# State products of the first quarter split straight from PSUM, other quarters by stacked products, and a new order

## The chip, the cores and the metric

One core of a Trainium2 chip runs the kernel. Its engines are PE (matrix multiplication), DVE (vector), ACT (scalar functions), POOL (general) and SP, which here issues the DMAs. The metric is the device time of one execution in microseconds; lower is better. Times given for a kernel are the median of several executions, and the profile is one more execution, recorded by the hardware.

## The reference

```python
# x: (8, 8, 512, 64)  state: (8, 8, 32, 64)   batch, head, rows, D
scores = scale * x @ state^T;   a  = softmax(scores);   xread = a @ state
scores2 = scale * state @ x^T;  a2 = softmax(scores2);  sread = a2 @ x
y = concatenate([xread, sread], axis=2)          # 544 rows a head
rows = y.transpose(0, 2, 1, 3).reshape(8 * 544, 512)
h = rows @ w_in                                  # 512 x 2048
g = maximum(h, 0) + log1p(exp(-abs(h)))          # softplus
out = g @ w_out                                  # 2048 x 512
```

`w_in` and `w_out` come as 64-bit floating point and are turned into 32-bit words on the chip.

## The kernel before

**The products.** The kernel does not compute xread. Because xread @ w_in is the sum over heads of a times (state times the head's 64 rows of w_in), it first makes the *state product* V = state @ w_in of each batch (256 rows, head by state row, by 2048 columns), and then the hidden tile h.b.f (128 columns of h for batch b, 512 rows) from V and the softmax a. Every factor is split into a high part, rounded to the fast matmul format, and a low part, the rest (`split`: the high part is a cast, L293 on ACT, the low part a subtraction, L309 on DVE); a product takes three matmuls (high-high, high-low, low-high). A hidden tile has two groups of heads, so six matmuls. Softplus (`s`) and another split (`gh`, `gl`) follow, and four output products of three matmuls (`m.b.f.c`) with tile f of w_out (`Wh`, `Wl`) add into accumulators of one PSUM bank each.

**Four quarters.** w_in is treated in four quarters c of 512 columns, four hidden tiles each. Quarter pieces of w_in are loaded (`Li`), converted by three steps (`ch` on ACT, `cu` and `cr` on DVE: a scaled high word, the low word's bits by L341 or by the pair L344 and L345, and their union, L349), and stored for later (`Sw`). For quarters 0 and 1 the state products come from plain 32-bit matmuls (`V0` for batches 0 and 1, `V1` for batches 2 and 3, 128 rows of two batches by two heads). Batches 0 and 1 are copied from PSUM into a buffer Vk (`va`) and then split (`vh`, `vl`); batches 2 and 3 are copied out (`ve`), stored to DRAM (`Sv`) and loaded again in another layout (`F`). Quarters 2 and 3, and batches 4 to 7 of all quarters, use *stacked products*: a head's rows of w_in are split into a high and a low half, stacked in one operand R (`Rh`, `Rl`, L370), and multiplied by the high and the low part of the states of four batches (`P`, two matmuls, fast format); the result is evicted (`pe`), stored (`Sp`, vd<-px) and loaded back (`F`, Vf<-vd).

**Attention.** For batches 0 and 1 the scores (`Q`) are plain 32-bit matmuls of z, a block layout of the state, and xT, x transposed. DVE transposes the scores in blocks (`A`, L457), takes maxima (`M`, L458), POOL or DVE subtracts (`Ms`, L460), ACT takes the exponential (`m`, L461), DVE sums, adds EPS and inverts (`N`, L464 to L466), POOL or DVE multiplies (`Nm`, L470), DVE transposes back (`D`, L471), and a split gives aH and aL. The row maxima (`E`, L479 and L480) and the row exponentials (`e`) serve sread alone, which is needed at the end (tile 8 of h).

**The order.** `PLAN` is an order written out: each step's name, its engine (V and W are DVE with one or two instructions for the low words, A and C are ACT, G POOL, T PE, S SP), and the number of the buffer or PSUM bank of what it makes. Every engine works through its own instructions in that order and waits for what each needs. The batches' hidden tiles run in turns: batch 0 tiles 0 to 3, batch 1 tiles 0 to 7, batch 0 tiles 4 to 11, batch 1 tiles 8 to 15, batch 0 tiles 12 to 15, then batch 2 and so on. Sixteen records of matmuls on zeros (`h.idle`, eight matmuls, WARM, L744) stand at the very start, and transposes of the identity (`w`, L604) fill some places of PE's order. z of batches 0 and 1 is cleared by POOL (`zn`, L544); its two halves are copied in from a loaded buffer zf (`zc`).

```python
rs = slice(64 * (q % 2), 64 * (q % 2) + 64)
for b in range(2):
    op(f"va.{k}.{b}", "AV", [f"vp.0.{k}"], [f"Vk.{b}.{c}:{i}"],
       lambda e, k=k, b=b, c=c, q=q, cs=cs, rs=rs, n=n:
       copy(e, page(f"Vk.{b}.{c}", 2, 512)[rs, q // 2, cs], at(f"vp.0.{k}")[64 * b:64 * b + 64, 0:n]))
```

Of the kernel before, what the change touches and what calls it, by code (L numbers as in the profile page):

```python
# [8 lines left out]
F32 = mybir.dt.float32  # L9
F32R = mybir.dt.float32r  # L10
I32 = mybir.dt.int32
I64 = mybir.dt.int64
# [7 lines left out]
P = 128  # L20
# [8 lines left out]
WARM = 8  # L29
TURNS = ((0, 0, 4), (1, 0, 8), (0, 4, 12), (1, 8, 16), (0, 12, 16))  # L30
PACKED = (2, 3)
# [3 lines left out]
Lt.0:S:0 Lz.0:S:1 zn.0:G:0 Li.0.1:S:2 Lq.1:S:3 Li.0.3:S:4 Lq.0:S:5 Li.0.0:S:6 Li.0.7:S:7 Lo.0:S:0 Lo.1:S:1 Li.0.2:S:8 zc.0.0:V: zc.0.1:V: Q.0.0:T:0  # L35
ch.0.1:C:9 cu.0.1:W:10 cr.0.1:V: Sw.0.1:S: ch.0.3:A:11 cu.0.3:V:12 V1.0.1:T:1 E.0.0:V: Q.0.1:T:2 ve.0.1:A:13 cr.0.3:V: Sv.0.1:S: A.0.0:V:14 zn.1:G:15
ch.0.0:A:16 Lz.1:S:17 Lt.1:S:1 cu.0.0:V:18 ch.0.7:A:19 M.0.0:V: V0.0.3:T:3 Sw.0.3:S: w.25:T:4 A.0.1:V:20 Li.0.6:S:21 va.0.3.1:A:2 Ms.0.0:G: w.26:T:5
va.0.3.0:A:3 Li.0.5:S:22 w.27:T:6 E.0.1:V: Li.0.4:S:23 w.28:T:7 m.0.0:A: M.0.1:V: e.0.1:A:24 cr.0.0:V: N.0.0:V: Ms.0.1:G: w.32:T:1 Sw.0.0:S: V1.0.0:T:4
ch.0.2:C:25 V0.0.1:T:5 ve.0.0:A:26 cu.0.2:W:27 V1.0.3:T:3 m.0.1:A: cu.0.7:V:28 cr.0.2:V: va.0.1.1:A: cr.0.7:V: ve.0.3:A:29 N.0.1:V: zc.1.0:A: Nm.0.0:G:
V1.0.7:T:6 Sw.0.7:S: zc.1.1:A: va.0.1.0:A: w.40:T:7 Sv.0.0:S: e.0.0:A:30 V0.0.7:T:2 Lo.2:S:4 cu.o0:V:31 V0.0.0:T:1 D.0.0:V:32 ve.0.7:A:33 Sw.0.2:S:  # L40
Nm.0.1:G: V0.0.2:T:4 va.0.7.1:A: Sv.0.7:S: va.0.0.0:A: V1.0.2:T:3 va.0.0.1:A: Li.1.1:S:5 cu.o1:V:34 va.0.2.0:A: Q.1.1:T:5 ah.0.0:A:35 D.0.1:V:36
vh.0.0:G:37 va.0.7.0:A: al.0.0:V:38 ah.0.1:A:39 cu.0.6:V:40 ch.0.6:A:41 vl.0.0:V:42 Q.1.0:T:7 Sv.0.3:S: va.0.2.1:A: Li.1.3:S:6 cr.0.6:V: ch.0.4:A:43
cu.0.4:V:44 Lo.3:S:7 cu.0.5:V:45 ch.0.5:A:46 cr.0.4:V: Sw.0.6:S: ch.o0:A:47 cr.0.5:V: Sw.0.4:S: V0.0.4:T:0 ch.o1:A:48 A.1.0:V:49 al.0.1:G:50 V0.0.5:T:6
va.0.4.0:A: A.1.1:V:51 V0.0.6:T:1 va.0.4.1:A: va.0.5.0:A: M.1.0:V: h.0.1:T:2 va.0.5.1:A: ch.o2:A:52 va.0.6.0:V: Li.1.2:S:8 Ms.1.0:G: M.1.1:V:
va.0.6.1:A: vh.0.1:A:53 h.0.0:T:4 cr.o0:V: Li.1.0:S:9 vl.0.1:V:55 V1.0.4:T:0 cr.o1:V: s.0.1:A:54 h.0.2:T:6 s.0.0:A:56 cu.o2:V:57 ve.0.4:V:58 Ms.1.1:G:
wh.0:A:59 gh.0.0:A:60 V1.0.6:T:1 wl.0:V:61 h.0.3:T:2 wh.1:A:62 gl.0.0:V:1 gh.0.1:A:2 s.0.2:A:9 cr.o2:V: m.0.0.2:T:4 ve.0.6:A:4 wl.1:V:11 wh.2:A:6
# [210 lines left out]
def width(buf):  # L257
# [5 lines left out]
    if kind in ("xT", "po"):  # L263
        return 4
    if kind in ("o8", "x", "xs", "Wf", "Vk", "aa"):
        return 2
    return 2 if kind == "w8" and at[0] != "0" else 1


def rounded(buf):  # L270
# [543 lines left out]
```

## Time and profile before

| | us |
|---|---|
| median of 3 runs (671.3 to 672.15) | 672.12 |
| profiled execution | 673.18 |
| its span, first to last instruction | 671.4 |
| PE busy | 659.2 (98%) |
| DVE busy | 417.0 (62%) |
| ACT busy | 425.0 (63%) |
| POOL busy | 16.5 (2%) |

The page cuts the span into 40 slices of 16.8 us; each digit is the busy share of a slice in tenths. PE's and DVE's rows, with the other rows of the page left out:

```profile
PE   7899999999999999999999999999999999999997
...
DVE  4999999836987896354854476446736666322210
```

A timeline row has its start and its length in us, the engine, the line, the operation, out<-in by names, shapes and a count; in brackets stands how long the engine was idle before it and what ended that. A matmul's length in such a row includes its way through the pipeline, so lengths overlap; the distance between starts is what a matmul costs in a full stream. A plain 32-bit matmul shows as two records.

### The profile page before, as it was taken

The numbers are of one execution on the slowest core, as the hardware profiler recorded it, in microseconds if no ns is written. First come the engines' busy times: TensorE is split into PE (matmuls) and PEld (weight loads), VectorE is DVE, ScalarE is ACT, GpSimd is POOL, SyncE is SP. The second block draws the span as 40 slices with busy tenths as digits, with TensorE's granted clock in tenths as the row PEclk, the third lists the DMA queues.
The fourth block names the chain that finished last, engine by engine and source line by source line (L and its number), as shares of the span: only waits on it lengthen the run. The fifth ranks groups of instructions, "written<-read, shape, count | busy, mean of one in ns | idle before, by whom it ended". The sixth has DMA issues, their size and how long they took to land.

```text
span 671.4 us, 8968 instructions
## 1 busy us (share of the span) xinstructions
PE 659.2 (98%) x3036; PEld 540.2 (80%) x3036; DVE 417.0 (62%) x802; ACT 425.0 (63%) x751; POOL 16.5 (2%) x21
## 2 busy tenths in 40 slices
PE   7899999999999999999999999999999999999997
PEld 5567778888888788888888888888888888988886
DVE  4999999836987896354854476446736666322210
ACT  3979998877877686563864467456845747324322
POOL 2430000000000000000000000000000000000000
PEclk9999999999999999999999999999999999999999
DMA  8849677675063434521341122312073312103001
GB/s 323 311 169 314 257 239 219 237 241 169 30 207 121 143 125 142 183 93 32 94 160 38 31 79 89 108 36 90 27 232 104 109 55 79 48 18 78 1 0 63
DMA packets 50638, 85.54 MB, mean 127 GB/s; under 512 B 7072, under 2 KB 28576, under 8 KB 49568
## 3 DMA queue, kind: packets, MB, share of 16 engines
q1 hardware_dynamic: 50592, 84.96, 38.8%
q8 instruction: 24, 0.39, 0.2%
q14 instruction: 22, 0.18, 0.1%
HBM read 57.15 MB, written 27.79 MB: 127 GB/s over the span
## 4 chain that ended last, share of the span: by engine, by line
PE 90%; ACT 5%; DVE 2%; DMA 2%; issue 1%; SPq 0%; DVEq 0%; ACTq 0%
PE acc L312 52%; PE h L312 28%; PE pp L312 3%; PE rp L312 2%; PE qp L312 2%; PE sc L312 1%; ACT Vk L293 1%; PE gp L498 1%; DMA x<-in_xn_dram 1%; PE vp L312 1%; DVE wf L349 1%; DMA zf<-in_zp_dram 1%; ACT t L611 1%; ACT gH L293 0%; ACT L611 0%
## 5 line engine op out<-in xcount | busy, mean ns | idle before, releaser
L312 PE MATMUL acc<-Wh,gH 128*128 128x512 f32 x544 | 213.3, 392 | 0.0
L312 PE MATMUL acc<-Wl,gH 128*128 128x512 f32 x544 | 212.1, 390 | 0.3 <-DVE Wl L309 0.3
L312 PE MATMUL acc<-Wh,gL 128*128 128x512 f32 x544 | 211.7, 389 | 0.0
L309 DVE TENSOR_TENSOR gL<-t,gH 128x512 fp32r<-128x512 f32 x136 | 93.2, 693 | 172.1 <-ACT gH L293 168.5
L611 ACT ACTIVATE t<-h 128x512 f32<-128x512 f32 x136 | 80.2, 598 | 171.9 <-PE h L312 168.8
L312 PEld LDWEIGHTS acc<-Wh,gL 128*128 128x128 f32 x544 | 102.1, 188 | 21.5
L312 PEld LDWEIGHTS acc<-Wl,gH 128*128 128x128 f32 x544 | 102.2, 188 | 21.1 <-DVE Wl L309 0.7
L312 PEld LDWEIGHTS acc<-Wh,gH 128*128 128x128 f32 x544 | 102.2, 188 | 20.8 <-issue 0.2
L312 PE MATMUL h<-aH,Vh 128*128 128x512 f32 x256 | 101.7, 397 | 0.3 <-DVE xq L524 0.3
L312 PE MATMUL h<-aH,Vl 128*128 128x512 f32 x256 | 99.9, 390 | 0.0
L312 PE MATMUL h<-aL,Vh 128*128 128x512 f32 x256 | 99.7, 389 | 0.0
L293 ACT CAST gH<-t 128x512 fp32r<-128x512 f32 x136 | 83.1, 623 | 3.1 <-PE acc L312 0.6
L312 PEld LDWEIGHTS h<-aH,Vh 128*128 128x128 f32 x256 | 48.0, 188 | 12.2 <-issue 1.4
L312 PEld LDWEIGHTS h<-aH,Vl 128*128 128x128 f32 x256 | 48.0, 188 | 10.7 <-DVE Vl L309 0.5
L312 PEld LDWEIGHTS h<-aL,Vh 128*128 128x128 f32 x256 | 48.1, 188 | 9.8 <-issue 0.2
L309 DVE TENSOR_TENSOR Vl<-Vf,Vh 128x512 fp32r<-128x512 f32 x56 | 38.2, 683 | 6.2 <-ACT Vh L293 5.0
L293 ACT CAST Vh<-Vf 128x512 fp32r<-128x512 f32 x56 | 34.5, 620 | 0.1
L312 PE MATMUL h<-sreadT,uH 128*128 128x256 f32 x128 | 23.4, 283 | 0.0
L293 ACT COPY o<-acc 128x512 f32<-128x512 f32 x26 | 14.6, 587 | 13.3 <-PE acc L312 12.7
L312 PE MATMUL vp<-wf,QZ 128*128 128x256 f32 (+1 forms) x48 | 17.1, 469 | 5.3 <-DVE wf L349 5.3
L309 DVE TENSOR_TENSOR xs<-x,xs 128x512 fp32r<-128x512 f32 x32 | 20.4, 685 | 1.9 <-ACT xs L293 1.9
L575 DVE TENSOR_TENSOR sc<-qp,qs 64x512 f32<-64x512 f32 x24 | 16.4, 683 | 8.0 <-ACT qs L573 7.5
(113 smaller groups left out, 759.4 us busy)
## 6 DMA issues: line engine op xcount, KB each, us to landing
vd<-px SPq DMA_DIRECT2D x48, 256.0 KB, 2.1
Vf<-vd SPq DMA_DIRECT2D x192, 64.0 KB, 2.0
xT<-in_xt_dram SPq DMA_DIRECT2D x8, 1024.0 KB, 5.5
o<-in_w_out_dram SPq DMA_DIRECT2D x16, 512.0 KB, 4.6
x<-in_xn_dram SPq DMA_DIRECT2D x16, 512.0 KB, 4.5
w<-in_w_in_dram SPq DMA_DIRECT2D x12, 512.0 KB, 5.7
out_dram<-o SPq DMA_DIRECT2D x24, 256.0 KB, 2.1
Wf<-wsc SPq DMA_DIRECT2D x32, 128.0 KB, 2.8
```

The source lines that it names most:

```text
L293: nc.scalar.copy(dst, src)
L309: lambda e: eng(e).tensor_tensor(r(dlo()), src(), dhi(), ALU.subtract))
L312: nc.tensor.matmul(dst, lhs, rhs, start=start, stop=stop)
L349: nc.vector.scalar_tensor_tensor(u, page(f"h2.{key}", n).bitcast(I32), 3, u, ALU.logical_shift_left, ALU.bitwise_or)
L498: nc.tensor.transpose(at(f"gp.{b}.{g}")[:, P * c:P * c + P], at(src)[:, P * c:P * c + P], at("ident"))
L575: lambda e, kj=kj, sc=sc, j=j: nc.vector.tensor_tensor(at(sc)[64 * j:64 * j + 64], at(f"qp.{kj}")[0:64], at(f"qs.{kj}")[0:64], ALU.add))
L611: lambda e: nc.scalar.activation(at(f"t.{k}"), at(f"h.{k}"), AF.Softplus))
```

## The change

- *Quarter 0 of batches 0 and 1.* The matmuls of `V0` and `V1` now belong to batch 0 and batch 1, and put 64 rows each (two heads of one batch) into the lower and the upper half of one PSUM bank, so that the bank holds what Vk held. `vh` and `vl` read the bank itself; Vk and the `va` copies are gone. The four conversions are 512 wide (two 128-row pieces by 256 columns) where there were eight of 256.
- *Everything else by stacked products.* Quarter 1 of batches 0 and 1, and quarters 0 and 1 of batches 2 and 3, now come from stacked products, through px, vd and Vf. Stacked products grow from 48 to 64; `ve` and `Sv` are gone, and batches 2 and 3 no longer come from plain matmuls. Quarter 1's R is made from the converted words at once; only quarter 0 is loaded again (`Lr`) for it.
- *Attention of batches 0 and 1.* xT is loaded in two halves; z's halves are loaded straight into the cleared block layout, so the loads wait for POOL's memset and `zc` is gone. ACT copies the scores from PSUM to the buffer e2 (`qk`), and the row maxima and exponentials read that copy, later.
- *The order.* WARM is 12 in place of 8 (24 records). `PLAN` is new throughout.

```diff
-WARM = 8
+WARM = 12
-            if c in PACKED:
-                for o in range(2):
-                    stack(c, 2 * q + o, o, f"wf.{k}", wf)
-                continue
-            for z in range(2):
-                op(f"V{z}.{k}", "T", [f"QZ.{z}", wf], [f"vp.{z}.{k}"],
-                   lambda e, z=z, k=k, q=q, n=n: mm(at(f"vp.{z}.{k}")[:, 0:n], page(f"QZ.{z}", 4, P)[:, q],
-                                                    page(f"wf.{k}", n), True, True))
...
+    for i in range(4):
+        j, x = i // 2, i % 2
...
+        for b in range(2):
+            def product(e, b=b, j=j, k=k, x=x):
+                for y in range(2):
+                    mm(page(f"vp.{b}.{j}", 2, 256)[64 * y:64 * y + 64, x],
+                       page("QZ", 4, P)[:, 2 * x + y, 64 * b:64 * b + 64], page(f"wf.{k}", 2, 256)[:, y], True, True)
+
+            op(f"V{b}.{k}", "T", ["QZ", wf], [f"vp.{b}.{j}:{x}"], product)
+    for c in range(1, 4):
+        for q in range(4):
...
+            for o in range(2):
+                stack(c, 2 * q + o, o, f"wf.{k}", wf)
...
-        for s4 in range(2) if c in PACKED else (1,):
+        for s4 in range(2):
...
+                direct = b < 2 and c == 0
+                if direct:
+                    ins = [f"vp.{b}.{j}:{x}" for x in range(2)]
+                    src = lambda b=b, j=j: page(f"vp.{b}.{j}", 2, 256)
...
+                load(f"Lz.{b}.{j}", [f"z.{b}:{j}c"], lambda b=b, j=j: page(f"z.{b}", 4, P)[:, j::2, 64 * j:64 * j + 64],
+                     lambda b=b, j=j: io.zp[b][:, j::2], [f"z.{b}:0"])
...
+                op(f"qk.{k}", "A", [sc], [f"e2.{k}:s"], lambda e, k=k: nc.scalar.copy(at(f"e2.{k}"), at(f"sc.{k}")))
```

Of the new order three places are shown. The first is DVE's start (sc scores, T their transposed softmax, mx maxima, sm sums, nm row maxima, wf converted weights). Before, from the first union of words on:

```order
L349 SCALAR_TENSOR_TENSOR wf_1_134<-h_0_1_132,wf_1_134 128x256
L341 TENSOR_SCALAR wf_3_141<-w_0_3_113 128x256
L479 TENSOR_REDUCE nm<-sc_0_129 128x1
L480 TENSOR_SCALAR nm<-nm 128x1
L349 SCALAR_TENSOR_TENSOR wf_3_141<-h_0_3_139,wf_3_141 128x256
L457 STREAM_TRANSPOSE T_0_154<-sc_0_129 128x512
L341 TENSOR_SCALAR wf_0_164<-w_0_0_117 128x256
L458 TENSOR_REDUCE mx<-T_0_154 128x16
```

DVE's start with the change, from the first transposed scores on:

```order
L442 STREAM_TRANSPOSE T_1_129<-sc_1_119 128x512
L443 TENSOR_REDUCE mx<-T_1_129 128x16
L442 STREAM_TRANSPOSE T_0_149<-sc_0_131 128x512
L443 TENSOR_REDUCE mx<-T_0_149 128x16
L449 TENSOR_REDUCE sm<-T_1_129 128x16
L450 TENSOR_SCALAR sm<-sm 128x16
L451 RECIPROCAL sm<-sm 128x16
L340 TENSOR_SCALAR wf_0_173<-w_0_0_125 128x512
```

The softmax moved ahead of the conversions, and the row maxima moved out of this stretch.

The second is PE's order just ahead of batch 1's first hidden tile (vp state products, gp transposes for sread, acc output products, pp stacked products). Before:

```order
L312 MATMUL vp_1_1_544<-wf_1_453,QZ_111 128x512
L312 MATMUL vp_1_2_552<-wf_2_455,QZ_115 128x512
L312 MATMUL vp_1_0_565<-wf_0_539,QZ_115 128x512
L498 MATMUL gp_0_575<-ident,e_0_0_247 128x128 x4
L312 MATMUL vp_1_3_586<-wf_3_557,QZ_115 128x512
L312 MATMUL vp_1_2_597<-wf_2_455,QZ_111 128x512
```

The same place with the change:

```order
L311 MATMUL vp_0_456<-wf_0_173,QZ 64x256 x2
L311 MATMUL vp_0_456<-wf_1_184,QZ 64x256 x2
L311 MATMUL acc_0_3_343<-Wh_293,gH_1_336 128x512
L311 MATMUL acc_0_3_343<-Wl_307,gH_1_336 128x512
L311 MATMUL acc_0_3_343<-Wh_293,gL_1_362 128x512
L311 MATMUL pp_1_4_477<-R_4_433,KH_1_408 128x512
L311 MATMUL pp_1_4_477<-R_4_433,KL_1_427 128x512
```

Quarter 1's plain state products are gone from here, and the first stacked product of quarter 1 stands ahead of batch 1's first hidden tile.

The third is SP's queue with the change, where quarter 1's state products go out and come back (px evicted products, vd their place in DRAM, 1_73 for batches 0 to 3 and 1_74 for 4 to 7, Vf the loaded layout, o and w pieces of w_out and w_in). No such rows stood there before:

```order
L302 DMA vd_1_73<-px_1_6_655 128x512
L299 DMA Vf_2_671<-vd_1_73 32x2x256
L302 DMA vd_1_73<-px_1_0_661 128x512
L302 DMA vd_1_73<-px_1_2_669 128x512
L302 DMA vd_1_74<-px_1_7_673 128x512
L299 DMA Vf_2_693<-vd_1_73 32x2x256
L299 DMA Vf_2_671<-vd_1_73 32x2x256
L299 DMA Vf_2_693<-vd_1_73 32x2x256
L299 DMA Vf_3_708<-vd_1_73 32x2x256 x2
L299 DMA Vf_2_671<-vd_1_73 32x2x256 x2
L299 DMA Vf_2_693<-vd_1_73 32x2x256 x2
L299 DMA o_6_755<-in_w_out_dram 128x512
```

Stores and loads of the first and second quarter now follow each other on SP, with loads of weights behind them.

More of the change, by code (lines that the diff above doesn't have):

```diff
@@ L264, in width @@
         return 4
-    if kind in ("o8", "x", "xs", "Wf", "Vk", "aa"):
+    if kind in ("o8", "x", "xs", "Wf", "aa"):
         return 2
-    return 2 if kind == "w8" and at[0] != "0" else 1
+    return 2 if kind == "w8" else 1
 def rounded(buf):
@@ L415, in graph @@
-    for c in range(4):
-        for q in range(4 if c not in PACKED else 0):
+    load("Lq", ["QZ"], lambda: page("QZ", 4, P), lambda: io.zq[:, 0])
+    for i in range(4):
+        j, x = i // 2, i % 2
+        k, cs = f"0.{i}", slice(256 * j, 256 * j + 256)
+        load(f"Li.{k}", [f"w8.{k}"], lambda k=k: page(f"w8.{k}", 2, 512).bitcast(I64),
+             lambda x=x, cs=cs: io.w_in[0, 2 * x:2 * x + 2, :, cs].rearrange("q p n -> p q n"))
+        wf = convert(k, f"w8.{k}", f"wf.{k}", 512, None)
+        store(f"Sw.{k}", [wf], lambda x=x, cs=cs: io.wsc[0][256 * x:256 * x + 256, cs].rearrange("(q p) n -> p q n", q=2),
+              lambda k=k: page(f"wf.{k}", 2, 256), [f"D:wsc.0.{2 * x + y}.{256 * j}" for y in range(2)])
+        for b in range(2):
[4 more added lines that the diff above has]
+            op(f"V{b}.{k}", "T", ["QZ", wf], [f"vp.{b}.{j}:{x}"], product)
@@ L417, in graph @@
+    for c in range(1, 4):
+        for q in range(4):
             k = f"{c}.{q}"
-            load(f"Lr.{k}", [f"wr.{k}"], lambda k=k: at(f"wr.{k}"), lambda c=c, q=q: io.wsc[c][P * q:P * q + P, :],
-                 [f"D:wsc.{c}.{q}.{x}" for x in ((0, 256) if c == 0 else (0,))])
+            load(f"Li.{k}", [f"w8.{k}"], lambda k=k: page(f"w8.{k}", 1024).bitcast(I64), lambda c=c, q=q: io.w_in[c, q])
+            wf = convert(k, f"w8.{k}", f"wf.{k}", 512, None)
+            store(f"Sw.{k}", [wf], lambda c=c, q=q: io.wsc[c][P * q:P * q + P, :], lambda k=k: page(f"wf.{k}", 512), [f"D:wsc.{c}.{q}.0"])
@@ L420, in graph @@
             for o in range(2):
-                stack(c, 2 * q + o, o, f"wr.{k}", f"wr.{k}")
+                stack(c, 2 * q + o, o, f"wf.{k}", wf)
+    for q in range(4):
+        load(f"Lr.0.{q}", [f"wr.0.{q}"], lambda q=q: at(f"wr.0.{q}"), lambda q=q: io.wsc[0][P * q:P * q + P, :],
+             [f"D:wsc.0.{q}.{x}" for x in (0, 256)])
+        for o in range(2):
+            stack(0, 2 * q + o, o, f"wr.0.{q}", f"wr.0.{q}")
     for b in range(B):
@@ L427, in graph @@
                 k, cs = f"{b}.{2 * c + j}", slice(256 * j, 256 * j + 256)
-                kept = b < WHOLE and c not in PACKED
-                V = f"Vk.{b}.{c}" if kept else f"Vf.{k}"
-                if kept:
-                    ins = [f"{V}:{i}" for i in (range(4 * j, 4 * j + 4) if c == 0 else range(4))]
-                    src = lambda V=V, cs=cs: page(V, 2, 512)[:, :, cs]
-                else:
-                    n = 4 if b >= 4 or c in PACKED else 2
-                    h = P // n
-                    ins = [f"{V}:{x}" for x in range(n)]
+                direct = b < 2 and c == 0
@@ L437, in graph @@
+                if direct:
+                    ins = [f"vp.{b}.{j}:{x}" for x in range(2)]
+                    src = lambda b=b, j=j: page(f"vp.{b}.{j}", 2, 256)
+                else:
+                    V = f"Vf.{k}"
+                    ins = [f"{V}:{x}" for x in range(4)]
                     src = lambda V=V: page(V, 2, 256)
[L438 to L446 removed]
+                    for x in range(4):
+                        load(f"F.{k}.{x}", [f"{V}:{x}"], lambda V=V, x=x: page(V, 2, 256)[NS * x:NS * x + NS],
+                             lambda b=b, c=c, x=x, cs=cs: io.Vd[b // 4, c].rearrange(
+                                 "(g hh) n f -> hh n g f", hh=4)[x, NS * (b % 4):NS * (b % 4) + NS, :, cs],
+                             [f"D:vd.{b // 4}.{c}.{x}", f"D:vd.{b // 4}.{c}.{4 + x}"])
@@ L540, in graph @@
         whole = b < WHOLE
-        load(f"Lz.{b}", [f"zf.{b}"], lambda b=b: page(f"zf.{b}", 4, 64), lambda b=b: io.zp[b])
-        load(f"Lt.{b}", [f"xT.{b}"], lambda b=b: page(f"xT.{b}", 4, S), lambda b=b: io.xt[b])
+        if not whole:
+            load(f"Lz.{b}", [f"zf.{b}"], lambda b=b: page(f"zf.{b}", 4, 64), lambda b=b: io.zp[b])
+        if whole:
+            for g in range(2):
+                load(f"Lt.{b}.{g}", [f"xT.{b}:{g}"], lambda b=b, g=g: page(f"xT.{b}", 4, S)[:, 2 * g:2 * g + 2], lambda b=b, g=g: io.xt[b, :, 2 * g:2 * g + 2])
+        else:
+            load(f"Lt.{b}", [f"xT.{b}"], lambda b=b: page(f"xT.{b}", 4, S), lambda b=b: io.xt[b])
         if whole:
@@ L713, in attention_then_softplus_mlp @@
     for c in range(4):
-        io.Vd[0, c] = dp.tile([H, P, 512] if c in PACKED else [P, 4, 512], F32, tag=f"vd0_{c}", name=f"vd0_{c}")
-        io.Vd[1, c] = dp.tile([H, P, 512], F32, tag=f"vd1_{c}", name=f"vd1_{c}")
+        for s4 in range(2):
+            io.Vd[s4, c] = dp.tile([H, P, 512], F32, tag=f"vd{s4}_{c}", name=f"vd{s4}_{c}")
     ident = cp.tile([P, P], F32, name="ident")
```

452 lines of the change are left out of this document (210 added, 242 removed).

## The prediction

> **What bounds the kernel now.** After the page's slices (shown above: PE full nearly everywhere, DVE only early) I read the table by stretches, then the timelines and groups of the first 60 us.
>
> ```profile
> 12.50:27.70 15.20, 11.24 (x46) 7.29 (x45) 13.80 (x31) 11.79 (x31) 6.52 (x6) 1.00 0.99 346
> 27.70:54.40 26.70, 25.06 (x100) 17.39 (x98) 26.10 (x46) 22.94 (x43) 8.39 (x7) 1.00 0.62 213
> ...
> 230.00:667.00 437.00, 436.98 (x2073) 365.51 (x2072) 226.57 (x433) 241.15 (x424) 0.00 (x0) 1.00 0.26 81
> ```
> Each row is a stretch (us), its length, then the busy times of PE, weight loads, DVE, ACT and POOL, and the granted clock. From 230 us on PE idles 0.02 us of 437; before 27.7 us it idles 4 of 15, while DVE is nearly full. So an edit counts only if it changes PE's amount of work or PE's waits, and the waits lie early.
>
> ```profile
> 6.31 3.75 PE L312 MATMUL sc<-xT,z 128*128 128x512 f32 x4 [1.48 <-DVE z L297]
> ...
> 20.07 1.89 PE L312 MATMUL vp<-wf,QZ 128*128 128x256 f32 x8
> 21.80 3.60 PE L312 MATMUL sc<-xT,z 128*128 128x512 f32 x8
> ...
> 29.31 0.40 PE L312 MATMUL h<-aH,Vh 128*128 128x512 f32 x1
> ...
> 54.45 0.47 PE L312 MATMUL h<-aH,Vh 128*128 128x512 f32 x1
> ```
> PE's waits here are for weights that DVE converts (4.0 us to 29.2 and 1.3 later, in rows further down) and, once, for z (1.48). At 29.31 the second hidden tile starts (the first, six matmuls, is then issued); 54.45 is batch 1's first. The end of the first hidden tile is my landmark. The time is when it comes, plus PE's work left after it, plus PE's waits after it, plus an unchanged tail.
>
> **Term 1: when the first hidden tile ends.** Once the scores are there, DVE hardly rests. The rows of DVE's order at the start stand with the change. The softmax now comes ahead of the conversions, the row maxima (L479, L480) are gone from here, and eight conversions of 256 columns became four of 512. DVE's pace:
>
> ```profile
> 13.50 0.72 DVE L457 STREAM_TRANSPOSE T<-sc 128x512 f32<-128x512 f32 x1 [0.79 <-PE sc L312]
> 14.14 0.65 DVE L479 TENSOR_REDUCE nm<-sc 128x1 f32<-128x512 f32 x1
> ...
> 39.01 0.69 DVE L464 TENSOR_REDUCE sm<-T 128x16 f32<-128x512 f32 x1
> ...
> 40.11 0.66 DVE L349 SCALAR_TENSOR_TENSOR ow<-h_o,ow 128x512 int32<-128x512 int32 x1
> 40.69 1.54 DVE L309 TENSOR_TENSOR gL<-t,gH 128x512 fp32r<-128x512 f32 x1
> 42.15 0.67 DVE L464 TENSOR_REDUCE sm<-T 128x16 f32<-128x512 f32 x1
> ...
> 49.47 0.41 DVE L341 TENSOR_SCALAR wf<-w 128x512 int32<-128x512 int32 x1
> 49.80 0.68 DVE L309 TENSOR_TENSOR Vl<-Vk,Vh 128x512 fp32r<-128x512 f32 x1
> 50.41 0.68 DVE L349 SCALAR_TENSOR_TENSOR wf<-h,wf 128x512 int32<-128x512 int32 x1
> ```
> Starts lie 0.60 us apart for a 128x512 elementwise instruction, 0.64 for a transpose or maximum, 0.33 for a shift of low words; sum, EPS and reciprocal take 1.10 together (39.01 to 40.11). The gL at 40.69 held DVE 1.46, not 0.60, because POOL multiplied beside it: 0.86 for such a meeting.
>
> ```profile
> 1.05 3.78 PE L744 MATMUL h_idle<-idle 128*128 128x128 f32 x16 [1.05 <-DVE idle L742]
> ```
> ```profile
> 1.25 0.99 POOL L544 MEMSET z<- 128x512 f32 x2
> 12.80 1.05 POOL L460 TENSOR_TENSOR T<-T,mx 128x512 f32<-128x512 f32 x1 [10.57 <-DVE mx L458]
> ```
> ```profile
> 40.34 1.34 POOL L470 TENSOR_TENSOR T<-T,sm 128x512 f32<-128x512 f32 x1 [9.15 <-DVE sm L466]
> ```
> ```profile
> 10.10 0.69 DVE L479 TENSOR_REDUCE nm<-sc 128x1 f32<-128x512 f32 x1 [0.21 <-PE sc L312]
> ```
> ```profile
> 14.70 0.63 ACT L461 ACTIVATE T<-T 128x512 f32<-128x512 f32 x1
> ```
> The idle matmuls grow from 16 records to 24, so they end near 6.3 us. The state loads now wait on SP for POOL's memset (done by 2.24), and the other loads queue behind them, 1 us at most, with half of xT already in flight; xT and z were both there by 6.3 us before, so I let the first scores start at 6.2. Four such records took 3.75 us at 6.31, eight took 3.60 at 21.80: 0.9 each at the slow pace, 0.44 at the fast. At the fast pace the scores end at 7.95, and DVE starts 0.25 later, at 8.2. A transpose and a maximum (1.4), POOL's subtraction (1.05), ACT's exponential (0.63) and three hand-overs of 0.1: the first sum starts at 11.6. From there DVE runs without a rest to the last low part that the first hidden tile reads: two sums (2.2), four shifts (1.32), eight elementwise (four joins, a multiplication, two aL, a Vl: 4.8, and 0.09 for the last to end), four transposes or maxima (2.56), one meeting with POOL (0.86), 11.8 in all. It ends at **23.4**; five matmuls (1.13) and a hand-over later the tile is issued, at **24.6** against 29.31: **4.7 us earlier**. ACT's copies into Vk are gone from there, so ACT keeps up.
>
> The page gives a granted clock of 1.00 in every stretch, although the durations halve. By the Trainium skill ("TensorE: Matmul & The Clock Gate", Part 1) full clock comes after a window of about 3.4 us of sustained activity; the 24 records reach the scores without the 1.48 us gap of before, and by that rule the pace is fast before 8 us. Without it the first scores would be slow, which is the second rival.
>
> **Term 2: PE's work left after it.**
>
> ```profile
> 659.50 8.17 PE acc L312 x36
> ```
> ```profile
> L312 PE MATMUL vp<-wf,QZ 128*128 128x256 f32 x26 | 7.3, 408 | 4.0 <-DVE wf L349 4.0
> ```
> The first row, of the chain, gives 0.227 us a matmul: 1.36 a hidden tile, 0.68 an output product (three), 0.453 a stacked product (two). The second counts the quarter products' records up to the landmark, 26 of 32; 3 products (two records each) of 0.43 (four at 20.07 took 1.89 with their tail) and 8 of twice the columns, 0.86, are left: 8.2 us. After, two of the eight 64-row pairs are left. No row shows a weight of 64 columns; a half streams 256 columns like a quarter product, so it costs at most 0.43 and at least half of that, if two halves share the array. I take 0.43, the nearest row: 1.7 us. The last scores (1.7) are still to come too, and 16 more stacked products (48 to 64): 7.3. Together 10.7 against 8.2: **+2.5 us**.
>
> By the Trainium skill ("TensorEngine Tiling (Array Packing)", Key Properties) column tiles work in parallel, and a change of tiling drains the engine; by that the sum would be 0.9 less, plus two drains. No row of this case shows either.
>
> **Term 3: PE's waits after it.** Two of PE's groups from 29.3 to 54.44 before:
>
> ```profile
> L312 PE MATMUL acc<-Wh,gH 128*128 128x512 f32 x16 | 6.4, 401 | 0.0
> ...
> L312 PE MATMUL vp<-wf,QZ 128*128 128x512 f32 x12 | 6.0, 605 | 1.3 <-DVE wf L349 1.3
> ```
> 16 output products (10.9), six state products of 0.86 and three of 0.43 (6.5), three hidden tiles (4.1) and eight transposes (0.9) make 22.4 of 25.1 us: 2.8 lost. The rows of PE's order ahead of batch 1's first hidden tile, before and now, stand with the change. The stacked product (pp) between output products is new at this place; it reads the low rows of R, which stand behind 30 other pieces on DVE. PE gets there after 3 tiles, the scores, 14 output products and two pairs, 17.1 us: 41.7. DVE needs from 23.4: 18 elementwise (nine low parts of V, W and g, five joins, two subtractions, KL, R: 10.8), six shifts (2.0), four transposes or maxima (2.6), two sums (2.2), a row maximum (0.8): 18.4, and two meetings with POOL (1.7). It ends at 41.8 to 43.5, and with a hand-over PE waits 0.2 to 1.9 us; I take 1.5. Further on, the stacked products follow DVE's R rows closely, 0.6 more. 2.1 against 2.8: **-0.7 us**. The rest of the run keeps its order of engines, and DVE and ACT lose about as much work (Vk and ve copies) as they get (16 evictions of stacked products).
>
> Sum: -4.7 + 2.5 - 0.7 = **-2.9 us**. The profiled execution took 673.18 (span 671.4), so 670.3 by it; it was 1.06 above the median of the runs, 672.12, which gives 669.2. I forecast **669.4**.
>
> **Rivals.**
>
> ```profile
> vd<-px SPq DMA_DIRECT2D x48, 256.0 KB, 2.1
> Vf<-vd SPq DMA_DIRECT2D x192, 64.0 KB, 2.0
> ...
> vd<-ve SPq DMA_DIRECT2D x4, 256.0 KB, 5.9
> ```
> ```profile
> 56.32 1.52 SPq L303 DMA_DIRECT2D vd<-ve  x3
> ```
> *A round trip takes the place of the copies (slower).* The second quarter of batch 1's state products (hidden tiles 4 to 7) used to stay on chip; now it goes px to vd to Vf. Between the last stacked product it needs and its first tile PE has 10 output products and 7 stacked ones, 10.0 us. Eviction with its queue 1.2; from that store to the last load eight issues on SP (at most 0.5 each by the row of 56.32, 4.0, the landing of 2.1 within); landing 2.0; both splits 1.3: 8.5, covered. But stores among loads took 5.9 in this stretch of before: 1.2 + 5.9 + 0.5 + 5.9 + 1.3 = 14.8, PE idles 4.8, 674.2. It decides from landings of 3.5 us each. Against it: the weights' loads stand behind these in SP's order, shown with the change.
>
> *A slow start.* If z comes late or the scores run at 0.9 a record, they end 1.8 us later, the second scores as much again in part: 2.2 of the 4.7 go, 671.6. For it: before, the pace was slow until the second scores.
>
> *Halves in parallel.* 0.9 less: 668.5.
>
> *It does not do what it says:* the start hangs on DMA, not DVE. The weights of the first tile come after 2.9 MB; at 346 GB/s (the row of 12.5 to 27.7) that is 8.5 us, against conversions from 13 on. Little for it.
>
> **How the numbers follow.** Forecast, 0.56: 668.9 to 670.7 with the bounds of term 3. Parallel halves, 0.14. Slow start or late data, 0.18: 670.8 to 672.5. Round trip, 0.12: mostly 672 to 675. Time 669.4; range 667.0 (parallel halves with no wait at the stacked product) to 672.4. About 0.2% (1.3 us) is what a measurement of this kernel tells from no change; faster than 670.8: 0.70, within 0.2%: 0.20, slower than 673.5: 0.10.
>
> **What would show it.** Term 1: the second hidden tile starts near 24.6 and DVE has no rest from 11.6; the scores' four records take 1.8. Term 2: the page has 64 stacked products, and late 64-row records 0.22 apart. Term 3: PE's longest wait after 24 us is for R. I am wrong if PE waits for Vh or Vl of batch 1 behind Vf loads, or if the first scores start after 7 us.

## The result, and the profile after

The change makes the kernel slower: 679.83 us, the median of four runs (678.18 to 680.74), against 672.1 before; the ratio is 1.0115, 95% interval 1.0093 to 1.0137. The forecast was 669.4, with 0.70 for a time under 670.8. The profiled execution took 678.18 us with a span of 676.4.

The table by stretches for the kernel with the change, columns as in the prediction, and under it two rows of before for stretches that the prediction did not show:

```profile
12.50:27.70 15.20, 10.12 (x41) 5.27 (x42) 15.03 (x30) 9.55 (x18) 2.09 (x2) 0.89 1.04 373
27.70:54.40 26.70, 25.22 (x109) 18.84 (x107) 26.07 (x50) 26.24 (x46) 2.35 (x2) 1.00 0.49 182
54.40:100.00 45.60, 43.02 (x191) 33.85 (x192) 39.93 (x75) 40.03 (x71) 0.00 (x0) 1.00 0.86 302
100.00:230.00 130.00, 128.21 (x580) 103.19 (x579) 106.94 (x209) 99.43 (x177) 0.00 (x0) 1.00 0.59 198
```
```profile
54.40:100.00 45.60, 45.29 (x207) 36.01 (x206) 44.57 (x89) 45.14 (x79) 0.00 (x0) 1.00 0.81 269
100.00:230.00 130.00, 130.00 (x592) 107.39 (x591) 101.87 (x195) 99.55 (x170) 0.00 (x0) 1.00 0.51 172
```

PE, which idled 0.3 us between 54 and 230 us, now idles 4.4 there. From 54 to 100 us, where most of that falls, DVE and ACT are less busy than before. The forecast had looked at the first 54 us and let the rest stand.

PE's timeline with the change, at the places that the prediction named:

```profile
6.55 1.96 PE L311 MATMUL sc<-xT,z 128*128 128x512 f32 x4
...
15.99 1.72 PE L311 MATMUL vp<-wf,QZ 128*64 128x256 f32 x8 [4.09 <-DVE wf L348]
17.64 3.08 PE L311 MATMUL sc<-xT,z 128*128 128x512 f32 x4
20.65 1.95 PE L311 MATMUL vp<-wf,QZ 128*64 128x256 f32 x16
...
25.95 0.39 PE L311 MATMUL h<-aH,Vh 128*128 128x512 f32 x1
...
44.09 0.50 PE L311 MATMUL pp<-R,KH 128*128 128x512 f32 x1 [1.37 <-DVE R L369]
...
46.03 0.39 PE L311 MATMUL h<-aH,Vh 128*128 128x512 f32 x1
```

The second hidden tile starts at 25.95 (29.31 before, 24.6 forecast), batch 1's first at 46.03 (54.45 before). At 46 us the change is 8.4 us ahead in time, though with more work left; it ends 5.0 us behind: the last matmul record starts at 672.26, before at 667.27.

To see where, I sum PE's waits: the distance between the starts of neighbouring matmul records less the usual distance for their shape (0.227 us for 512 columns in the fast format, 0.109 for a pair record of 64 rows, 0.430 and 0.215 for a plain 32-bit record of 512 and 256 columns), between hidden tiles that both kernels have (tiles go by their number, whatever runs between them). Each number is from one profile.

| PE's waits, us | before | change |
|---|---|---|
| second hidden tile to batch 1's first | 2.8 | 2.0 |
| batch 1's first to batch 0's fifth (46 to 96 us with the change) | 1.2 | 4.8 |
| on to batch 1's ninth (96 to 140) | 0.5 | 2.1 |
| on to batch 1's thirteenth (140 to 171) | 0.0 | 2.7 |
| on to the end | 1.5 | 1.1 |

Landmark -3.36, PE's work after it +1.64, its waits after it +6.70 (6.0 to 12.7): +5.0, which is what the two profiled executions differ by. The medians differ by 7.7; that varies from run to run, since the mean granted clock was 0.997 in the two faster runs of the change (678.18 and 679.35) and 0.991 and 0.992 in the two slower (680.30 and 680.74).

The chain that ended last, with the change, shows what those waits hang on (start, length, what):

```profile
63.04 0.46 SPq L299
...
68.03 0.43 SPq L299
...
68.50 3.64 DMA o<-in_w_out_dram
...
72.22 0.68 ACT h_o L331
72.90 0.48 ACT px L292
73.42 0.74 PE pp L311 x2
...
75.18 7.75 DMA o<-in_w_out_dram
83.33 0.43 SPq L299
83.81 0.43 SPq L299
84.28 8.36 DMA vd<-px
92.83 0.70 DVE Vl L308
```

SP issues DMAs, a load of w_out comes late, ACT stands on its conversion, and PE on the eviction (px) queued behind it on ACT. Then a load of 7.75 us, and a *store* that lands 8.36 us after its issue, on which DVE's Vl waits. Neither is a load of Vf. Before, this chain ran mostly through ACT from 54 us on and, from 74 us, through PE alone.

SP's queue with the change, a stretch of the run while SP stood, and two rows that wait at the far end:

```profile
32.30 0.33 SPq L299 DMA_DIRECT2D sk<-in_stk_dram  x1
51.17 0.33 SPq L302 DMA_DIRECT2D wsc<-wf  x1
51.54 0.43 SPq L299 DMA_DIRECT2D o<-in_w_out_dram  x1
...
157.79 0.79 SPq L299 DMA_DIRECT2D xT<-in_xt_dram  x1
```
```profile
40.00:51.00 11.00, 9.63 (x45) 7.05 (x44) 10.79 (x22) 10.65 (x20) 1.05 (x1) 1.00 0.00 1
```
```profile
92.83 0.69 DVE L308 TENSOR_TENSOR Vl<-Vf,Vh 128x512 fp32r<-128x512 f32 x1 [2.05 <-DMA vd<-px]
```
```profile
167.06 0.50 PE L311 MATMUL qp<-xh,z 128*128 128x512 f32 x1 [1.06 <-ACT xh L292]
```

From 32.30 to 51.17 SP stood on one store, which waits for DVE's conversion of wf.1.1; the DMA engines moved 1 GB/s from 40 to 51 us, with loads behind that store whose buffers were free. Before, the longest such stand was 9.2 us:

```profile
37.39 0.36 SPq L300 DMA_DIRECT2D x<-in_xn_dram  x1
46.54 0.33 SPq L303 DMA_DIRECT2D wsc<-wf  x1
```

My theory Q was: the change's written order puts DMAs behind others on SP that are not yet due, and PE pays later. Its rivals were R, the latency of px to vd to Vf itself; W, too much work for ACT and DVE; and C, the clock, which the table by stretches gives as 0.89 in the first row.

### The profile page after: what moved, and what is told of

Same layout as the page of the kernel before. It is cut to its first block, busy times and chain, and to the rows that moved or that the text cites. A ratio compares the mean times of both kernels' runs of the same rounds, so it can differ in the third digit from the quotient of the medians.

```text
span 676.4 us, 9038 instructions
## 1 busy us (share of the span) xinstructions
PE 659.9 (98%) x3062; PEld 539.7 (80%) x3062; DVE 411.1 (61%) x788; ACT 417.0 (62%) x731; POOL 7.1 (1%) x13
## 4 chain that ended last, share of the span: by engine, by line
PE 83%; DVE 5%; DMA 4%; ACT 4%; SPq 2%; issue 1%; ACTq 0%; DVEq 0%
PE acc L311 48%; PE h L311 26%; PE pp L311 3%; PE rp L311 2%; DMA o<-in_w_out_dram 2%; PE qp L311 2%; SPq L299 2%; DMA xT<-in_xt_dram 1%; DMA vd<-px 1%; PE gp L483 1%; PE h_idle L737 1%; ACT px L292 1%; ACT gH L292 1%; ACT t L604 1%; PE sc L311 1%
## 5 line engine op out<-in xcount | busy, mean ns | idle before, releaser
L311 PEld LDWEIGHTS h<-aL,Vh 128*128 128x128 f32 x256 | 48.1, 188 | 10.7 <-DVE aL L308 0.9
L308 DVE TENSOR_TENSOR Vl<-Vf,Vh 128x512 fp32r<-128x512 f32 x60 | 40.7, 684 | 14.2 <-ACT Vh L292 7.4
L292 ACT CAST Vh<-Vf 128x512 fp32r<-128x512 f32 x60 | 36.9, 620 | 9.6 <-DMA Vf<-vd 7.9
L311 PE MATMUL pp<-R,KH 128*128 128x512 f32 x64 | 26.1, 408 | 2.5 <-DVE R L369 1.8
L292 ACT COPY px<-pp 128x512 f32<-128x512 f32 x41 | 23.1, 590 | 3.4 <-PE pp L311 2.6
L311 PE MATMUL pp<-R,KL 128*128 128x512 f32 x64 | 25.1, 391 | 0.0
L311 PEld LDWEIGHTS h<-sreadT,uH 128*128 128x128 f32 x128 | 20.6, 191 | 0.8
```

Source lines behind the costliest of these rows:

```text
L292: nc.scalar.copy(dst, src)
L308: lambda e: eng(e).tensor_tensor(r(dlo()), src(), dhi(), ALU.subtract))
L311: nc.tensor.matmul(dst, lhs, rhs, start=start, stop=stop)
```

## The experiments

All are edits of the change. Each median is of 5 to 12 executions. Ratios are to the kernel before, run on the same chip beside them; its medians there were 672.19 us (e1 to e4), 672.10 (e5 to e8), 672.46 (f1 to f3), 672.19 (f4) and 671.78 (g1, g2).

| run | median, us | ratio | interval |
|---|---|---|---|
| e1_loads | 676.57 | 1.0064 | 1.0052 to 1.0076 |
| e2_store | 679.76 | 1.0115 | 1.0098 to 1.0132 |
| e3_xt | 675.66 | 1.0054 | 1.0042 to 1.0066 |
| e4_warm | 679.31 | 1.0108 | 1.0091 to 1.0125 |
| e5_copy | 678.48 | 1.0102 | 1.0086 to 1.0117 |
| e6_two | 678.07 | 1.0105 | 1.0079 to 1.0132 |
| e7_queue | 674.13 | 1.0031 | 1.0020 to 1.0043 |
| e8_all | 672.88 | 1.0019 | 1.0010 to 1.0027 |
| f1_copy | 672.75 | 1.0005 | 0.9996 to 1.0014 |
| f2_dve | 674.37 | 1.0028 | 1.0018 to 1.0037 |
| f3_warm | 675.04 | 1.0033 | 1.0022 to 1.0043 |
| f4_dve2 | 673.39 | 1.0022 | 1.0013 to 1.0032 |
| g1_cut | 673.36 | 1.0022 | 1.0013 to 1.0031 |
| g2_cut | 680.61 | 1.0123 | 1.0102 to 1.0144 |

**SP's order.** The lines cut from `PLAN`, here and below, leave out the steps between ("...").

```diff
-Sw.1.1:S: ... Lo.5:S:4 ... Sp.0.1.4:S: ... Li.2.1:S:5 ... F.1.3.2:S: ... Lo.6:S:8 ... Lo.7:S:0
+Lo.5:S:4 Li.2.1:S:5 Lo.6:S:8 Lo.7:S:0 Sw.1.1:S: ... Sp.0.1.4:S: ... F.1.3.2:S: ...
```

> Edit: four loads (w_out tiles 5, 6, 7 and one quarter piece of w_in, 2 MB) stand ahead of the store of wf.1.1 on SP instead of behind it. Theory Q (SP's single queue): with the change SP stood 18.9 us (32.30 to 51.17) on that store, DMA moved nothing from 40 to 51, and the loads then collided with the round trip; so here DMA is busy after 40, ACT's two idle spells for w_out (1.63 us before 72.22, 1.00 before 74.37) go, PE's waits of 0.71 at 72.5 and 0.49 at 76.3 go with them, and the time falls by 1 to 2.5 us from 679.8. Theory R (the latency of px to vd to Vf itself) and theory W (ACT and DVE have too much to do from 46 to 170): less than 0.5 us.

3.3 us, somewhat more than expected. In this run ACT's conversion of w_out's tile 6 follows without a pause, and PE has no idle time from 70 to 88 us (0.87 with the change). Two stretches and a row of this run:

```profile
40.00:51.00 11.00, 9.63 (x45) 7.03 (x44) 10.79 (x22) 10.63 (x20) 1.05 (x1) 1.00 0.27 108
...
70.00:88.00 18.00, 18.00 (x80) 14.39 (x79) 17.28 (x34) 16.55 (x29) 0.00 (x0) 1.00 0.94 316
```
```profile
70.79 0.68 ACT L319 ACTIVATE h_o<-o 128x512 f32<-128x512 f32 x1
```

The same with the change:

```profile
70.00:88.00 18.00, 17.13 (x74) 13.29 (x73) 16.12 (x31) 15.25 (x27) 0.00 (x0) 1.00 1.00 358
```
```profile
72.22 0.68 ACT L331 ACTIVATE h_o<-o 128x512 f32<-128x512 f32 x1 [1.63 <-DMA o<-in_w_out_dram]
```

PE's waits from 46 to 96 us fall from 4.8 to 2.3. Q holds here, W does not: ACT and DVE had the same work.

> Edit: only two of the four loads of the first experiment (w_out tile 5, one piece of w_in) stand ahead of the store of wf.1.1; w_out tiles 6 and 7 stay behind the twelve loads of Vf, which wait for stores of px. If standing on wf.1.1's store was the cause, most of the 3.3 us of the first experiment comes (2 to 3.3 us). If the round trip of quarter 1, on whose stores SP stands from 60 to 68 us, was the cause, ACT still waits for w_out tile 6 near 72, the waits of 0.7 and 0.5 us at 72 to 77 stay and less than 1.5 us comes.

The median is 1.8 us lower but the interval covers the change's, so the two loads' own gain is open. The interval lies just above the first experiment's, so tiles 6 and 7 of w_out, which stand behind the Vf loads, carry a part of the gain. How large it is stays open: 1.5 of 3.3 us by the medians, 0.41 of 0.51% by the ratios. ACT still waits for them:

```profile
73.13 0.67 ACT L319 ACTIVATE h_o<-o 128x512 f32<-128x512 f32 x1 [2.33 <-DMA o<-in_w_out_dram]
```

> Edit: the store of px.1.1.5, evicted near 70 us but issued at 84.28 behind three loads of 512 KB, stands with the other stores of quarter 1 instead. Theory Q: DVE's idle 2.05 us at 90.8 (Vl.0.3 waits for the buffer that this store reads, landing 92.64) goes, PE's wait of 1.54 before the fourth matmul of h.0.7 goes, and the time falls by 1 to 1.5 us from 679.8. Theory R: Vl waits for the loads of Vf and the wait stays; less than 0.3 us.

```diff
-Sp.1.1.1:S: ... Li.3.1:S:5 ... Lx.1.0:S:1 ... Li.3.3:S:10 Sp.1.1.5:S:
+Sp.1.1.1:S: Sp.1.1.5:S: ... Li.3.1:S:5 ... Lx.1.0:S:1 ... Li.3.3:S:10
```

The wait for Vl went, as Q says, but nothing was gained: other waits stand in its place, and in this profile the wait for xT was longer than in the change's.

```profile
86.80 0.50 PE L299 MATMUL acc<-Wl,gH 128*128 128x512 f32 x1 [0.50 <-DVE Wl L296]
...
168.40 0.49 PE L299 MATMUL qp<-xh,z 128*128 128x512 f32 x1 [2.29 <-ACT xh L280]
```
```profile
168.00:173.00 5.00, 4.37 (x12) 3.24 (x13) 3.55 (x6) 4.11 (x8) 0.00 (x0) 0.66 0.74 236
```

The second row matters for the next run: after 2.29 us of idle the granted clock fell, 0.66 over 5 us, so up to 1.7 us of clock are lost on top of the wait.

> Edit: the load of batch 2's xT (1 MB), issued at 157.79 behind some twenty stores and loads, stands 40 us earlier on SP. Theory Q: the first scores of batch 2 no longer wait (1.22 and 0.50 us before and after 167), the time falls by 1.2 to 1.7 us from 679.8. Rival W: ACT's casts of xT come no earlier since ACT is full, less than 0.4 us.

```diff
-Lz.2:S:42 Lt.2:S:1
+Sw.0.0:S: Lt.2:S:1 ... Lz.2:S:42
```

4.2 us, more than twice the waits in the change's profile (1.7). A part of the difference agrees with what the store's run showed: the idle time at 167 us varies (1.06 with the change, 2.29 there), and a long one can bring a slow stretch with it. With xT early, four of five runs had a mean clock of 0.997 and none was below 0.995. Those four are still 2.7 us faster on average than the change's two at 0.997, so about 1 us of the gain is not accounted for.

> Edit: the three moves on SP together (four loads ahead of wf.1.1's store, the store of px.1.1.5, batch 2's xT), all else as in the change. Theory Q: the gains add, 3.3 and 4.2 us and the rest of the wait before h.0.7, so 671.5 to 672.8, no slower than before the change; PE's waits after batch 1's first hidden tile, 10.7 us in the change's profile, fall to about 4, and no stretch of half clock is left but the first. Rival: the waits move to another place and the sum stays above 674.

5.7 us of the change's loss come back; the gains do not add fully, and 2 us remain. The waits after batch 1's first hidden tile fall from 10.7 to 7.4, not to 4. It is not the clock (C) either: at a mean clock of 0.997 the change took 678.2 and 679.4 us, this run 673.1, 673.2 and 673.5. Q is the main cause and not the whole.

**The round trip.** The chain above let me say in an expectation that SP "stands" from 60 to 68 us on loads of Vf that wait for stores. Two runs cut that dependence, with every transfer kept; hidden tiles 4 to 7 of batches 0 and 1 are then computed without their right state products.

```diff
+                        cut = b < 2 and c == 1
...
+                             (lambda b=b, x=x: io.xt[b, NS * x:NS * x + NS, 0:2, 0:256]) if cut else
...
-                             [f"D:vd.{b // 4}.{c}.{x}", f"D:vd.{b // 4}.{c}.{4 + x}"])
+                             [] if cut else [f"D:vd.{b // 4}.{c}.{x}", f"D:vd.{b // 4}.{c}.{4 + x}"])
```

> Edit: the same 16 loads cut loose in the change itself (679.83 us). Theory Q: SP no longer stands from 60 to 68 us on loads that wait for stores, w_out's tile 6 and 7 arrive before ACT asks for them, the wait of 0.7 us at 72.5 goes, and 1 to 2 us are gained, as the second half of the first experiment did (3.3 less 1.8); the rest stays (the store of wf.1.1, batch 2's xT). Theory R: 4 us or more. If neither, under 0.7 us.

> Edit: the run with three SP moves and the copies behind the exponentials (f1_copy, 672.75 us), but the 16 loads of Vf of quarter 1 for batches 0 and 1 read as many bytes of xT instead of vd, so they no longer wait for stores of px; the products of these hidden tiles are therefore left without their right V. Theory R (the round trip's latency is what is still missing): 1 to 2.5 us less, 670.3 to 671.7. Theory Q (with SP's order mended the round trip is covered by PE's other work): less than 0.5 us, 672.3 or more.

Neither gained: 680.61 against 679.83, and 673.36 against 672.75. My reading was wrong. The loads are issued at the same pace with and without the dependence, 0.49 us each; first the cut run, then the change:

```profile
62.88 5.34 SPq L287 DMA_DIRECT2D Vf<-in_xt_dram  x11
68.26 0.90 SPq L287 DMA_DIRECT2D o<-in_w_out_dram  x2
```
```profile
63.04 5.42 SPq L299 DMA_DIRECT2D Vf<-vd  x11
68.50 0.90 SPq L299 DMA_DIRECT2D o<-in_w_out_dram  x2
```

ACT still waits for w_out in g2_cut:

```profile
72.01 0.68 ACT L319 ACTIVATE h_o<-o 128x512 f32<-128x512 f32 x1 [1.48 <-DMA o<-in_w_out_dram]
```

So R falls for these tiles: what makes w_out late is its place behind twelve issues, whether or not they wait for stores. What the added transfers cost by their number and bytes, which both runs keep, was not tried. That g1_cut reads slightly slower than its base (1.0022 against 1.0005) lies for about half in the kernel before (671.78 beside one, 672.46 beside the other); the other half, 0.6 us between the medians, I cannot explain.

**The clock.**

> Edit: 36 more transposes of the identity in PE's idle stretch before its first state product (11.9 to 16.0 us). Theory C (clock): the granted clock stays at 1.00 from 16 to 20 us (0.61 and 0.53 with the change), the second scores' four records take about 1.9 instead of 3.08 us, the spans of the runs agree within 1 us, and the median falls by 1.5 to 2.5 us, although the first hidden tile comes no more than 0.2 us earlier, since it waits for DVE. Rival: DVE alone sets that stretch, the median moves by less than 0.5 us, and the spread from 678.2 to 680.7 has another cause.

```diff
+w.0:T:6 w.1:T:7 ... V0.0.0:T:0
```

The stretch at 16 us went, the second hidden tile stayed (25.92), and the median fell 0.5 us with overlapping intervals: the rival holds, the first slow stretch stands beside DVE's work. The spread stayed too (678.09 to 682.59), because in this kernel such stretches also come elsewhere:

```profile
16.00:20.00 4.00, 3.18 (x15) 1.16 (x13) 3.93 (x8) 2.23 (x4) 1.05 (x1) 1.00 1.03 410
...
95.00:99.00 4.00, 4.00 (x12) 3.17 (x11) 3.65 (x9) 3.81 (x8) 0.00 (x0) 0.57 0.49 183
```

**The copy of the scores.** In the change DVE's first transposes started 0.03 us after ACT's copies of the same bank ended:

```profile
9.16 0.72 DVE L442 STREAM_TRANSPOSE T<-sc 128x512 f32<-128x512 f32 x1 [8.16 <-ACT e L552]
...
11.24 0.72 DVE L442 STREAM_TRANSPOSE T<-sc 128x512 f32<-128x512 f32 x1 [0.64 <-ACT e L552]
```

> Edit: ACT's copy of the first two scores stands behind DVE's transpose of the same scores in the order, instead of ahead of it. Theory K (the transposes start only when the copy ends: 9.16 and 11.24 us, 0.03 after the copies' ends): the first transpose starts near 8.6, all of DVE's start and the second hidden tile come 0.5 to 1.2 us earlier (25.95 to about 25.1), and the time falls by as much, to about 679.0. Rival: two engines reading one bank slow each other whatever the order, or the copy is then late for nobody; the second hidden tile moves by less than 0.2 us.

```diff
-qk.0.1:A:3 A.0.1:V:2 ... qk.0.0:A:5 A.0.0:V:6
+A.0.1:V:2 qk.0.1:A:3 ... A.0.0:V:6 qk.0.0:A:5
```

The first transpose came 0.4 us earlier (8.76), yet the second hidden tile only 0.05. Now the copy waits for the transpose, and ACT's exponential, ready at 11.3, stands behind it:

```profile
11.66 0.59 ACT L540 COPY e<-sc 128x512 f32<-128x512 f32 x1 [1.57 <-DVE T L430]
12.15 0.63 ACT L434 ACTIVATE T<-T 128x512 f32<-128x512 f32 x1
```

The median is 1.35 us lower, with overlapping intervals. So the rows show two readers of one PSUM bank one after the other, in whichever order is written. The Trainium skill ("PSUM — Partial Sum Buffer", PSUM bank collisions raise a hardware error) says that a ScalarE read and a VectorE read of one bank collide, unarbitrated, and must be guarded; the waits here agree.

> Edit: the three moves on SP and the copy behind the transpose. Theories Q and K together: 670.5 to 672.0, that is 0.1 to 0.2% faster than before the change. Rival to K: as the run without it, 672.

> Edit: the three moves on SP, and ACT's copies of the first two scores behind ACT's first exponential and behind the second piece's conversion, so that they hold neither DVE's transposes nor the exponentials. Theory K in its second form (one bank's readers run one after the other in the written order, and behind the transpose the copy held the exponential by 0.8 us): the first sum on DVE starts near 12.0 (12.59 with the change, 12.81 with the copy right behind the transpose), the second hidden tile comes 0.4 to 0.7 us earlier than in the change at an equal start of the scores, and the median is 0.3 to 0.8 us below the 672.9 of the run with copies right behind. Rival: the weights' landing or PE's slow clock from 16 us sets the second hidden tile, which stays at 25.8 or later.

```diff
-m.0.1:A: ... ch.0.0:A:7 m.0.0:A: ... ch.0.1:A:9
+m.0.1:A: qk.0.1:A:3 ... ch.0.0:A:7 m.0.0:A: ... ch.0.1:A:9 qk.0.0:A:5
```

The lines are f1_copy's. With three SP moves and the copy right behind the transpose: 1.0019. At a mean clock of 0.997 this run's eight executions have a median of 672.7, so at equal clock the moved copy is worth some 0.5 us beside the 673.2 of e7_queue.

With the copies behind the exponentials the first sum starts at 12.23 and the second hidden tile at 25.59. Counted from the start of the second scores, on which DVE's second transpose hangs (8.60 us with the change, 8.86 here), both come 0.6 us earlier than with the change, as theory K in its second form said. The time is 1.0005, level with before; but the medians of e8_all and f1_copy lie only 0.13 us apart, and the ratios differ because the kernel before read 672.10 beside one and 672.46 beside the other. None of these versions is faster than the kernel before.

**DVE's order at 42 us.**

> Edit: as the run before it, and DVE's work ahead of batch 1's first hidden tile cut to what that tile needs: two row maxima (and one row exponential on ACT) go to their like near 84 us, a low part of K and two of R go behind Vl, and the first stacked product behind the second of batch 1's tiles. Theory D (DVE's order sets the wait for R of 1.5 us and batch 1's start): batch 1's first hidden tile comes 1.5 to 2.2 us earlier (45.9 to about 44), the wait of 1.5 us for R goes and the one of 0.6 at 54 with it, and the median falls by 1.2 to 2.2 us, to 670 to 671.5, faster than before the change. Rival: DVE has no slack from 46 to 70 us, what is deferred is waited for there, and less than 0.5 us comes.

> Edit: on the run with three SP moves and the copies behind the exponentials: DVE's row maximum of batch 0 (0.7 us) and its row exponential on ACT go from 41 us to about 86, the one of batch 1 from 53 to about 103, one low part of R ahead of the second transpose, one low part of K behind POOL's multiplication, and the first stacked product behind batch 1's first hidden tile, with its eviction behind another ACT already had to do, so that ACT doesn't stand on it (in the run before with these moves ACT stood 1.77 us on that eviction, and the first softplus of batch 1 came 1 us later). Theory D: batch 1's first hidden tile at 43.4 to 44 (45.7), the first softplus of batch 1 at 47.6 to 48.2 (48.8), the waits of 1.5 and 0.6 us for R gone, median 670.8 to 672.0, at or below the kernel before. Rival: DVE and ACT are both full from 36 to 72 us, so that what is moved past batch 1's first tiles is waited for a little later; by 71 us the order of hidden tiles stands where it stood, median 672.4 to 673.2.

```diff
-... N.1.1:V: ... E.0.1:V: ... D.1.0:V:25 ... e.0.1:A: D.1.1:V:13 ... Rl.1.4:V: ... P.0.1.4:T:0 ... h.1.0:T:7
+... N.1.1:V: ... D.1.0:V:25 Rl.1.4:V: ... D.1.1:V:13 ... h.1.0:T:7 P.0.1.4:T:0 ... E.0.1:V: ... e.0.1:A:
```

The lines are f4_dve2's against f1_copy's. In both runs the wait of 1.5 us for R is gone and batch 1's first hidden tile starts at 43.44 and 44.10 (45.70 in f1_copy). Both are slower at the end. In f2_dve I had put the eviction of the stacked product where ACT stood on it:

```profile
47.34 0.59 ACT L280 COPY px<-pp 128x512 f32<-128x512 f32 x1 [1.77 <-PE pp L299]
```

In f4_dve2 that is mended, and at batch 1's fifth hidden tile only 0.3 us is left of the 1.6. From batch 1's first hidden tile to batch 0's fifth, PE's waits, summed as above, are 3.9 us in f4_dve2 against 1.7 in f1_copy: the wait has moved. f1_copy's own stretches speak for the rival: DVE and ACT are nearly full there, so PE's wait for R covers work that would be waited for a little later anyway.

```profile
36.00:46.00 10.00, 8.62 (x41) 6.21 (x40) 9.48 (x18) 9.81 (x20) 2.35 (x2) 1.00 0.68 270
46.00:56.00 10.00, 9.57 (x42) 7.41 (x41) 9.81 (x19) 9.76 (x17) 0.00 (x0) 1.00 0.14 53
```

> Edit: as the run before it, with 30 transposes of the identity in PE's idle stretch ahead of the first state product. Theory C: without the half-clock stretch at 16 us the runs agree better (granted clock 1.000 in most) and the median falls by 0.3 to 1.0 us. Rival, which the same edit on the change alone spoke for (0.5 us, with the second hidden tile unmoved): that stretch stands beside DVE's work and costs nothing, less than 0.3 us.

The clock was 1.000 or 0.999 in five of eight runs, and the median no lower than f2_dve's. The rival holds a second time.

## Why the prediction was wrong

*Term 1, the landmark (-4.7).* -3.4. The slow-start rival did not come: the first scores took 1.96 us at the fast pace and started at 6.55, not 6.2. Of the 1.35 us missing, 0.35 is that start, 0.6 the transposes' wait for ACT's copy, which the term left out (the copy stood in the diff, but I priced it at nothing without naming what it holds), and the rest DVE's row, 12.1 us for the 11.8 of the walk. The slow scores at 17.64 (3.08 us for four records) cost nothing here. The granted clock of 1.00 that the prediction found odd in the first stretches of before was no reading: that trace holds no clock record before 12.46 us, and the view then puts 1.00; with the change the first record, full clock, starts at 6.22 us, just ahead of the first scores.

*Term 2, the work left (+2.5).* +1.64. The halves do run in parallel: 16 records of 64 rows took 1.95 us from 20.65, with starts 0.109 us apart on average, so a pair (four records) costs 0.43 and the two that were left 0.86 in place of 1.7, as the rule of the Trainium skill on column tiles had it ("TensorEngine Tiling (Array Packing)", Key Properties); taking the upper bound mis-sized the term by 0.86.

*Term 3, the waits (-0.7).* Up to batch 1's first hidden tile it was right: 2.0 us against 2.1, with 1.37 idle for R against 1.5. The step that failed is its last sentence, "The rest of the run keeps its order of engines". That is true of the engines' shares of work (over the whole run DVE was busy 411.1 us against 417.0, ACT 417.0 against 425.0), but not of SP's order. PE's waits from there on grew from 3.2 to 10.7 us, and the term came out at +6.7: 7.4 of the 7.9 us by which the whole sum (-2.9 against +5.0) was off. Three moves on SP give back 5.7 us of the medians' 7.7 (5.5 at equal clock), and the moved copies 1.4 more (0.5 at equal clock).

*The rival on the round trip.* Its price (674.2) had the right sign, but its mechanism did not occur: cut loose, the loads gained nothing. Its condition, landings of over 3.5 us, was met (8.36 at 84.28), but by stores among 512 KB loads, and what waited was a buffer that the store still read, not the round trip. Neither sign of being wrong that I had named came: the first scores started at 6.55, and the Vl that PE waited for until 93.58 was batch 0's, behind a store. The signs looked at Vf's path and at the start, not at the rest of SP's queue.

*What is still open.* f1_copy, level with before, should by the forecast be 3 us faster. Its profile has the landmark 1.0 us late, term 2 0.9 better than forecast, and PE's waits after the landmark 2.4 above the forecast's, in many places of 0.1 to 0.6 us, which no run took apart.

## What to carry to other kernels

When an order is written anew, read the DMA queue's order as closely as PE's: for each DMA ask what stands ahead of it, when that is due, and which engine's in-order queue stops on it. A wait of PE while two other engines are nearly full may only cover their work: without it PE may wait for them a little later. A copy added for a later reader also holds the bank's other reader.

## What the hardware showed unexpectedly

- *A half-clock stretch can follow an idle time of PE of about 2 us.* Past 30 us, the profiles show five idle times of PE of 1.9 to 2.5 us. Four were followed by one stretch of half clock: 2.29 us (e2_store, to 168.40; 0.66 over 5 us), 2.44 and 1.89 us (e4_warm, to 93.94 and 169.65; 0.57 over 4 us each) and 2.03 us (e5_copy, to 166.23; 0.66 over 5 us). One was not: 2.36 us (g2_cut, to 167.73; 1.00 over 5 us); nor was the 1.4 us before 93.58 in the change. Each stretch is a loss of 1.7 us, as 3.4 us at half clock. The Trainium skill ("TensorE: Matmul & The Clock Gate", Part 1) ties half clock to a window of about 3.4 us; the length agrees, but idle times well under it were enough in four of five cases. So a wait of 2 us, where PE is the bound, can cost nearly 4.
- *A DMA's issue has a price of its own on SP.* Eleven loads of 64 KB took 5.34 us to issue with nothing to wait for, 0.49 each, while the DMA engines were busy 0.74 of that time (60 to 70 us, 224 GB/s, in the change).
